# Batch 0 of windowed attention kept in float32 with its turns on TensorE, and constant matmuls in TensorE's gaps before the first feed-forward chunk

## The chip, the cores and the metric

One NeuronCore of a Trainium2 chip runs the kernel. The core has five engines with instruction queues of their own: TensorE (PE, matrix products and transposes), VectorE (DVE), ScalarE (ACT), GpSimd (POOL) and SyncE (SP, which here issues every DMA), and 16 DMA engines. Matrix products are written to PSUM, 8 banks of 128 x 512 float32. The metric is the device time of one execution in microseconds (us); smaller is better.

## What is computed

Eight batches go through an attention with 8 heads of width 64 (512 local and 32 global tokens; a local token sees the 32 global ones and the local ones at most 32 away), then through a Fourier mixing and a feed-forward block. Cut to what matters:

```
s_g   = scale * q_g @ k_all.T ;  out_g = softmax(s_g) @ v_all      # 32 global rows
s_l   = [scale * q_l @ k_g.T , where(|i-j| <= 32, scale * q_l @ k_l.T, -1e9)]
out_l = softmax(s_l) @ [v_g, v_l]                                  # 512 local rows
x     = concat(out_g, out_l)  -> (8, 544, 512)
u     = x + real(fft(fft(x, axis=1), axis=2))
un    = (u - mean(u)) / sqrt(var(u) + 1e-6)
out   = u + relu(un @ w_ch1) @ w_ch2                               # 512 -> 2048 -> 512
```

All of it is held to float32. Most matrix products are made of three float16 products each (high by high, high by low, low by high), for which every operand is first split into a float16 high part and a float16 rest.

## The kernel before, in words

The work is cut into tasks, one method of `Kern` each. `Plan` holds the tasks with an engine, an assumed duration, inputs (`after`), buffers used and made, and a due time. `Plan.order` is a list scheduler: it plays the tasks through a model of the engines, and always starts the task that can start first, ties by class and due time. Due times are propagated back from the consumers and shifted by the table `BIAS`, whose entries were per kind of task and stage. The order that comes out is the order of each engine's queue; nothing is reordered on the chip. Each engine waits on semaphores at the instructions that need another engine's or a DMA's result.

The program has three parts, which overlap:

- **Weights.** 32 tiles of `w_ch1` and `w_ch2` arrive as float64 bit patterns (`w_load`, 512 KB each, L349) and are rebuilt and split on ACT, DVE and POOL (`w_abs`, `w_low`, `w_bits`, `w_join`, `w_hi`, `w_lo`; `w_join` is L373 and L374, `w_bits` L368). `w_scale` 4 needs all 32.
- **Attention**, per batch 4 pairs of heads (p), per pair 2 halves (i) of 256 rows, per half 2 quarters (u) of 128 rows. `scores` (L607 in float32 for batches 0 and 1, L610 in float16 after) writes one bank pair `S` of which there is one. `masked` (DVE, L620) adds the mask, takes the minimum of the negated scaled scores, and copies to `per` (pe). `exps` (ACT, L629), `p_hi` (ACT, L633) and `p_lo` (POOL, L637) make the two float16 parts; `turn` (L642) transposes them by DMA; `values` (PE, L655 and L657) multiplies with the split v (`v_mul`, `v_hi`, `v_lo`, `v_out`); `norm` (DVE, L668) divides; `x_out` (SP, L756) stores. The 32 global rows go the same way in `g_*` tasks, with a DMA transpose in `g_turn` (L714).
- **Fourier mixing** of a batch begins when all of it has been stored: `d_load` (SP, L810 to L812) reloads it, POOL folds it (`d_odd`, L825, to `d_even3`), ACT and DVE split it (`d_hi`, `d_lo`), PE does `d_first` (L920, L922) and `d_second` (L950, L952), and `d_df`, `d_addv`, `d_addp` add the result to a second copy loaded by `load_pair`.
- **Feed-forward** in 17 chunks of 256 rows, two for each batch and a last one of left-over rows. `l_stats` (DVE, L1003), `l_guess`, `l_un` (L1017), `l_hi` (ACT), `l_lo` (DVE, L1026) and `l_turn` (SP, L1032, a DMA transpose for each of two halves) make the split, turned rows `uh`. Then PE does `f_first` (L1058, 192 matmuls in a chunk) and `f_second` (L1076, 96 matmuls), with `f_hi` (L1063) and `f_lo` (L1067) in between.

The first chunk (c = 0) needs the first 256 rows of batch 0, so all of batch 0's attention, its Fourier mixing up to `d_addv` of kt = 0, and the first 16 weight tiles. The `S` bank is a single buffer:

```
        s["S", half] = S = self.psa.tile([P, 2, 512], F32, name="S", tag="A", bufs=1)
```

## Time and profile before

| | us |
|---|---|
| median of 3 runs (1038.67 to 1040.35) | 1039.77 |
| the profiled execution's own time | 1040.43 |
| its span, from the first to the last instruction | 1038.2 |
| TensorE busy in the span | 942.3 |
| VectorE, ScalarE, GpSimd busy | 554.3, 573.0, 592.3 |

The profile is of one execution. Its page gives the busy time of each engine, the span in 40 slices of 26 us, the chain of work that ended last, and groups of instructions by source line with their mean duration, and the idle time before them with what ended it. Rows of the timeline begin with the start and the duration in us. The granted TensorE clock is given as a share of its full speed. Rows of windows give a stretch, its length, and the busy us of PE, PEld (weight loads), DVE, ACT and POOL with instruction counts in brackets, then clock, DMA share and GB/s.

### The profile page before, as it was taken

Reading aid. Unit: us, or ns where it says so; the run is one execution under the profiler, and the core shown is the slowest. Engines: PE = TensorE matmul, PEld = TensorE weight load, DVE = VectorE, ACT = ScalarE, POOL = GpSimd, SP = SyncE. Lnnn points to the kernel's source line nnn. Section 1 sums busy time; section 2 is a strip of 40 time slices with the busy share of each in tenths; the row PEclk is TensorE's granted clock in tenths of the full one; section 3 lists DMA queues with packets and bytes.
Section 4 is the critical chain, followed back from the end, with each engine's and each line's share of the span. In section 5 each row is a group of like instructions: output and inputs, shape, how many; then the busy total and the mean of one; then the engine's idle time right before and its main releaser. Section 6 shows DMA issues by size and latency. Waiting matters only on the chain.

```text
span 1038.2 us, 24797 instructions
## 1 busy us (share of the span) xinstructions
PE 942.3 (91%) x9683; PEld 669.2 (64%) x9683; DVE 554.3 (53%) x1609; ACT 573.0 (55%) x1234; POOL 592.3 (57%) x848
## 2 busy tenths in 40 slices
PE   3854366999999999999999999999999999999996
PEld 2653255667677776677676676777676676767673
DVE  4786899256855485577557557573434324131111
ACT  5996687967686866787777478452122111111110
POOL 4786876896878777969968697781262011010000
PEclk9765556999999999999999999999999999999998
DMA  9999985636786939896795667674230202101000
GB/s 323 246 247 264 285 220 130 133 97 149 153 196 158 224 67 204 147 217 131 146 208 101 185 128 156 135 141 69 57 100 11 62 3 63 42 21 41 1 21 21
DMA packets 249309, 137.59 MB, mean 133 GB/s; under 512 B 200320, under 2 KB 222944, under 8 KB 249192
## 3 DMA queue, kind: packets, MB, share of 16 engines
q1 hardware_dynamic: 249192, 136.00, 56.7%
q8 instruction: 76, 1.25, 0.5%
q14 instruction: 41, 0.34, 0.1%
HBM read 65.10 MB, written 18.35 MB: 80 GB/s over the span
## 4 chain that ended last, share of the span: by engine, by line
PE 71%; DVE 10%; DMA 6%; POOL 5%; ACT 3%; issue 2%; SPq 1%; POOLq 0%; DVEq 0%; ACTq 0%
PE acc L1076 29%; PE ps L1058 29%; PE S L610 3%; DMA pl<-ph 2%; DVE pe L620 2%; PE bk L655 2%; PE psd L950 2%; PE bk L657 2%; PE S L607 2%; DMA raw<-in_moe_w_ch 1%; DVE ps L373 1%; PE psd L920 1%; DMA x<-xs 1%; DMA u<-xs 1%; DVE mx L368 1%
## 5 line engine op out<-in xcount | busy, mean ns | idle before, releaser
L1058 PE MATMUL ps<-uh,wh 128*128 128x256 f16 x3264 | 380.6, 273 | 0.1
L1076 PE MATMUL acc<-wh,h 128*128 128x512 f16 x1632 | 375.1, 379 | 0.8 <-DVE h L1067 0.8
L1058 PEld LDWEIGHTS <-wh 128*128 128x128 f16 x3264 | 315.2, 98 | 51.6 <-issue 0.4
L1076 PEld LDWEIGHTS <-h 128*128 128x128 f16 x1632 | 153.9, 98 | 165.3 <-DVE h L1067 2.0
L1063 ACT ACTIVATE h<-ps 128x512 f16<-128x512 f32 x136 | 80.6, 593 | 268.9 <-PE ps L1058 268.6
L1067 DVE SCALAR_TENSOR_TENSOR h<-ps,h 128x512 f16<-128x512 f32 x136 | 93.6, 688 | 240.3 <-ACT h L1063 240.2
L637 POOL TENSOR_TENSOR ph<-pe,ph 128x448 f16<-128x448 f32 x128 | 132.9, 1054 | 45.1 <-ACT ph L633 39.9
L629 ACT ACTIVATE pe<-pe,nm 128x224 f32<-128x224 f32 x256 | 101.7, 469 | 13.6 <-DVE nm L620 13.6
L620 DVE CUSTOM_DVE_ANT_0 pe<-S,msk,z 128x224 f32<-128x224 f32 x192 | 75.0, 446 | 25.3 <-PE S L610 20.4
L633 ACT ACTIVATE ph<-pe 128x448 f16<-128x448 f32 x128 | 69.3, 564 | 27.7 <-DMA pl<-ph 27.6
L655 PE MATMUL bk<-vN,pl 128*128 128x65 f16 x768 | 69.1, 202 | 13.6 <-DVE x L668 6.2
L974 POOL TENSOR_TENSOR u<-u,asm 128x257 f32<-128x257 f32 x16 | 13.2, 825 | 103.1 <-DMA u<-xs 95.4
L655 PEld LDWEIGHTS <-pl 128*128 128x128 f16 x768 | 60.3, 103 | 14.6 <-DMA pl<-ph 7.6
L657 PEld LDWEIGHTS <-pl 96*128 96x128 f16 x768 | 58.6, 103 | 10.4 <-issue 6.2
L657 PE MATMUL bk<-vB,pl 96*128 96x65 f16 x576 | 52.6, 202 | 0.0
L607 PE MATMUL S<-qk 64*128 64x192 f32 x128 | 30.3, 562 | 22.4 <-DVE nm L620 19.8
L556 POOL TENSOR_TENSOR vN<-vf,vN 128x640 f16<-128x640 f32 x32 | 44.3, 1388 | 9.7 <-ACT vN L552 9.5
L1081 DVE SCALAR_TENSOR_TENSOR u<-acc,ve,u 128x512 f32<-128x512 f32 x34 | 25.4, 748 | 30.9 <-PE acc L1076 30.9
L610 PEld LDWEIGHTS <-qT 64*128 64x128 f16 x1152 | 34.6, 94 | 9.8 <-issue 6.3
L441 POOL TENSOR_TENSOR wh<-wm,wh 128x512 f16<-128x512 f32 x32 | 36.9, 1158 | 6.5 <-ACT wm L434 4.7
L1022 ACT ACTIVATE unh<-un 128x512 f16<-128x512 f32 x34 | 21.2, 624 | 28.0 <-DVE un L1017 27.8
L610 PE MATMUL S<-kT,qT 64*128 64x192 f16 x576 | 36.2, 246 | 0.0
(199 smaller groups left out, 1475.1 us busy)
## 6 DMA issues: line engine op xcount, KB each, us to landing
qk<-in_qk SPq DMA_DIRECT2D x32, 512.0 KB
vf<-in_v SPq DMA_DIRECT2D x32, 320.0 KB
raw<-in_moe_w_ch SPq DMA_DIRECT2D x17, 512.0 KB
xs<-x SPq DMA_DIRECT2D x32, 256.0 KB
out<-u SPq DMA_DIRECT2D x16, 512.0 KB
x<-xs SPq DMA_DIRECT2D x24, 256.0 KB
u<-xs SPq DMA_DIRECT2D x24, 256.0 KB
rw<-in_moe_w_ch SPq DMA_DIRECT2D x8, 512.0 KB
```

The lines of the kernel that those rows point to most:

```text
L607: nc.tensor.matmul(ps, q[r, P * j:P * j + P], kg[r] if o else kw[r, k0:k0 + 192], start=True, stop=True)
L610: nc.tensor.matmul(ps, qT[r, a, j], kg[r, c] if o else kT[r, k0:k0 + 192], start=m == 0, stop=m == 2)
L620: nc.vector.tensor_tensor_reduce(self.per[(4 * p + j) % 4][:, h, 0:224], S[:, h, 224 * n:224 * n + 224], self.msk[:, j], z[:, 8:9], 3e38, ...
L629: nc.scalar.activation(pe[:, h, 0:224], pe[:, h, 0:224], AF.Exp, bias=nm[:, n, h:h + 1], scale=-1.0)
L633: self.nc.scalar.activation(ph[:, 0, :, 0:224], self.per[i % 4][:, :, 0:224], AF.Copy)
L637: self.nc.gpsimd.tensor_sub(ph[:, 1, :, 0:224], self.per[i % 4][:, :, 0:224], ph[:, 0, :, 0:224])
L655: nc.tensor.matmul(pv[:, j % 2, h], pl[:, 4 * a + 2 * h], vN[:, j, c, h, :], start=m == 0, stop=False)
L657: nc.tensor.matmul(pv[:, j % 2, h], pl[0:96, 4 * a + 2 * h + 1], vb, start=False, stop=m == 2)
L1058: nc.tensor.matmul(ps[:, q], wt[:, w, c0:c0 + P], uh[:, :, 4 * a + kt, :], start=n == 0, stop=n == 11)
L1063: self.nc.scalar.activation(h[:, 0], self.fps[c, fp], AF.Relu)
L1067: self.nc.vector.scalar_tensor_tensor(h[:, 1], self.fps.pop((c, fp)), 0.0, h[:, 0], op0=ALU.max, op1=ALU.subtract)
L1076: nc.tensor.matmul(self.acc_f[c, j], h[:, a, q, j * P:(j + 1) * P], self.w[1, f][:, w, :], start=f == 0 and a == 0 and w == 0, stop=f == 1 ...
```

## The change

- **Batch 0 in float32 throughout** (`NRV`). v is no longer scaled and split: `load_v` puts it into a tile with a column of ones, so in pieces of 64 floats for each row and head (for all batches), and `load_vb` loads the shifted copy that `v_out` made. `p_hi`, `p_lo` and `turn` of batch 0's 16 quarters are replaced by `p_turn`, four float32 transposes on PE into PSUM, and `p_copy`, a copy to SBUF on DVE or ACT in turns; `values_raw` does 4 float32 matmuls where there were 12 float16 ones. The same holds for the global rows (`g_turn_raw`, `g_copy`, `g_values_raw`).
- **Masks on TensorE for batches 0 and 1** (`NPM`): the mask is added in `S` by a matmul with a bfloat16 identity, `maxima` on DVE only reduces, and `exps_ps` on ACT reads `S` itself.
- **Fourier banks**: `d_first` and `d_second` take one of three banks in batch 0 (before: two in turn) and one of two after (before: one).
- **First turns on TensorE** (`NLT`): chunks 0 and 1 turn `un` by 4 transposes for each half (`l_pt`), and `l_hi`, `l_lo` split from PSUM into `uh`; the DMA transposes of these two chunks go.
- **Constant matmuls**: until the first `f_first`, the scheduler notes PE's idle time ahead of a task; the methods that open a bank first write up to 12 matmuls of the mask (448 columns or fewer) into the bank that the task then overwrites (`fill`).
- **Order**: assumed durations, `BIAS` (now per kind and stage and per unit of work, some 300 entries) and some sequence constraints are new, so the order on every engine is new.

```
+NRV = 1
+NPM = 2
+NLT = 2
...
+COLD = 1.15
+FILL = 0.24
...
+BIAS = {('load_consts', 0): -10, ('K', 0): 61, ('w_load', 0): 624, ('W', 0): -433, ('w_abs', 0): -2, ('w_low', 0): 180,
...
-                t.dur *= 1.5
+                t.dur *= COLD
+                t.idle = at - free[e]
...
+    def run(self, kern):
         for t in self.order():
+            kern.fills = min(int(t.idle / FILL), 12)
             t.fn(*t.args, *([t.alt] if len(t.alts) > 1 else []))
...
+        self.idh = c.tile([P, P], BF16, name="idh")
+        nc.vector.tensor_copy(self.idh, self.ident)
...
+        self.vf = [c.tile([P, 5, 2, D + 1], F32, name=f"vf{i}") for i in range(4)]
...
-        self.nc.sync.dma_start(s["vf"], self.vd[s["b"], s["hp"]])
+        self.nc.sync.dma_start(s["vf"][:, :, :, 0:64], self.vd[s["b"], s["hp"]][:, 0:5])
+
+    def load_vb(self, p):
+        s = self.st[p]
+        s["vb"] = self.vb[p % NVB]
+        s["v"] = (None, None, self.zc[:, 0:1])
+        self.nc.sync.dma_start(s["vb"][:, :, :, 0:64], self.vd[s["b"], s["hp"], 0:96, 5:8])
...
+        pm = int(s["b"] < NPM)
         s["S", half] = S = self.psa.tile([P, 2, 512], F32, name="S", tag="A", bufs=1)
...
+        self.fill(S[:, 0])
...
+                if pm > o:
+                    for h in range(2):
+                        nc.tensor.matmul(S[:, h, 224 * n:224 * n + 192], self.idh, self.msk[:, j, 0:192], start=False, stop=True)
+
+    def maxima(self, i):
+        nc, (p, half) = self.nc, divmod(i, 2)
+        s = self.st[p]
+        s["nm", half] = nm = self.p2.tile([P, 2, 2], F32, name="nm")
+        S = s["S", half][:, :, 0:448].rearrange("p h (n k) -> p n h k", n=2)
+        nc.vector.tensor_reduce(nm, S, axis=EX, op=ALU.max)
+        nc.vector.tensor_scalar_mul(nm, nm, self.zc[:, 8:9])
+
+    def exps_ps(self, i):
+        nc, (p, half) = self.nc, divmod(i, 2)
+        nm, S = (self.st[p].pop((n, half)) for n in ("nm", "S"))
+        for n in range(2):
+            pe = self.per[(4 * p + 2 * half + n) % 4]
+            for h in range(2):
+                nc.scalar.activation(pe[:, h, 0:224], S[:, h, 224 * n:224 * n + 224], AF.Exp, bias=nm[:, n, h:h + 1], scale=0.125)
 
...
+    def p_turn(self, i, alt):
+        p, j = divmod(i, 4)
+        t = self.bank(alt)
+        self.fill(t)
+        self.st[p]["pt", j] = t = t.rearrange("p (c q) -> p c q", c=4)
+        for h in range(2):
+            for k in range(2):
+                self.nc.tensor.transpose(t[:, 2 * h + k], self.per[i % 4][:, h, P * k:P * k + P], self.ident)
+
+    def p_copy(self, i):
+        p, j = divmod(i, 4)
+        self.st[p]["pl", j] = pl = self.p3.tile([P, 4, P], F32, name="pl")
+        self.copy(i % 2, pl, self.st[p].pop(("pt", j)))
+
+    def copy(self, on_act, o, i):
+        if on_act:
+            self.nc.scalar.activation(o, i, AF.Copy)
+        else:
+            self.nc.vector.tensor_copy(o, i)
+
+    def values_raw(self, i):
+        nc, (p, j) = self.nc, divmod(i, 4)
+        s = self.st[p]
+        pl = s.pop(("pl", j))
+        if j % 2 == 0:
+            s["pv"] = self.bk[:, 0:260].rearrange("p (n h d) -> p n h d", n=2, h=2)
+        pv = s["pv"][:, j % 2]
+        for h in range(2):
+            vb = s["vb"][:, j, h] if j < 3 else s["vf"][0:96, 4, h]
+            nc.tensor.matmul(pv[:, h], pl[:, 2 * h], s["vf"][:, j, h], start=True, stop=False)
+            nc.tensor.matmul(pv[:, h], pl[0:96, 2 * h + 1], vb, start=False, stop=True)
 
...
+        for c in range(5):
+            self.nc.tensor.transpose(t[c // 4][:, P * (c % 4):P * (c % 4) + P], self.pg[:, P * c:P * c + P], self.ident)
...
+    def fill(self, ps):
+
+        n = min(ps.shape[1], 448)
+        m = self.msk.rearrange("p j k -> p (j k)")[:, 0:n]
+        for _ in range(self.fills):
+            self.nc.tensor.matmul(ps[:, 0:n], self.idh[:, 0:ps.shape[0]], m, start=True, stop=True)
+        self.fills = 0
+
+    def bank(self, alt, b=0):
+        if alt == (1 if b else 2):
+            return self.psa.tile([P, 2, 512], F32, name="S", tag="A", bufs=1)[:, 0]
+        return self.ps.tile([P, 512], F32, name="psd", tag="tr" if b else f"acc{alt}")
+
...
+    def l_pt(self, c, j, alt):
+        L = self.L[c]
+        t = self.bank(alt)
+        self.fill(t)
+        L["pt", j] = t = t.rearrange("p (k q) -> p k q", k=4)
+        un = L.pop(("un", j))
+        for k in range(4):
+            self.nc.tensor.transpose(t[:, k], un[:, P * k:P * k + P], self.ident)
+
+    def l_hi_ps(self, c, j):
+        L = self.L[c]
+        if j == 0:
+            L["uh"] = self.p2.tile([P, 2, 8, P], F16, name="uh", tag="uh")
+        self.nc.scalar.activation(L["uh"][:, j, 0:4], L["pt", j], AF.Copy)
+
+    def l_lo_ps(self, c, j):
+        L = self.L[c]
+        self.nc.vector.tensor_sub(L["uh"][:, j, 4:8], L.pop(("pt", j)), L["uh"][:, j, 0:4])
...
+                add(("load_vb", p), SP, .4, self.load_vb, p, new=[vN], kb=150, seq=[("load_v", p)] + prev("load_vb"), **kw)
+                continue
...
+                if b < NPM:
+                    add(("masked", i), DVE, 1.15, self.maxima, i, after=[("scores", i)], use=[S], new=[nm], **kw)
+                    add(("exps", i), ACT, 1.59, self.exps_ps, i, after=[("masked", i)], use=[nm, S], new=pers, **kw)
...
+                    if rv:
+                        pt = ("A", "p", u)
+                        add(("p_turn", u), PE, .6, self.p_turn, u, after=[("exps", i)], seq=[("p_turn", u - 1)] if u else [], use=[per], new=[pt], alts=[["acc0"], ["acc1"], ["A"]], **kw)
+                        add(("p_copy", u), ACT if u % 2 else DVE, .6 if u % 2 else .69, self.p_copy, u, after=[("p_turn", u)], use=[pt], new=[pl], **kw)
+                        add(("values", u), PE, 1.0, self.values_raw, u, after=[("p_copy", u), ("load_v", p), ("load_vb", p)], seq=order, use=[pl, vN, vf, bk], **kw)
+                        continue
...
+            banks = [["tr"], ["A"]] if b else [["acc0"], ["acc1"], ["A"]]
...
+                if c < NLT:
+                    pt = ("A", "l", c, j)
+                    add(("l_pt", c, j), PE, .6, self.l_pt, c, j, after=[("l_un", c, j)], use=[un], new=[pt], alts=[["acc0"], ["acc1"], ["A"]], cls=4)
+                    add(("l_hi", c, j), ACT, .6, self.l_hi_ps, c, j, after=[("l_pt", c, j)], seq=sq, use=[pt] + ([uh] if j else []), new=[] if j else [uh], cls=4)
+                    add(("l_lo", c, j), DVE, .68, self.l_lo_ps, c, j, after=[("l_hi", c, j)], use=[pt, uh], cls=4)
+                    continue
```

The order of the built program at three places. First TensorE's queue at batch 0's second block of scores, before the change (S is the score bank, qk a tile of q and k, gr the global q and k, bk the bank of totals and values):

```order
L607 MATMUL S<-qk_96 128x192 x2
L607 MATMUL S<-gr,qk_96 128x32 x2
L607 MATMUL S<-qk_96 128x192 x2
L607 MATMUL S<-gr,qk_96 128x32 x2
L424 MATMUL bk<-accg,part 128x2
L398 MATMUL vm<-ident,mx_94 1x128
```

And now, with tile numbers and waits; S_235 is the second use of the score bank, msk and idh the mask and the bfloat16 identity, pe the exponentials, psd a bank to turn them in:

```order
L1029 LDWEIGHTS idh_64 [waits DVE_49]
L1029 MATMUL S_235<-msk_63,idh_64 128x448 [waits Activation_49]
...
L648 MATMUL S_235<-qk0_97 128x192 x2
L654 LDWEIGHTS idh_64
L654 MATMUL S_235<-msk_63,idh_64 128x192
...
L648 MATMUL S_235<-gr_162,qk0_97 128x32 x2
L711 MATMUL psd_269<-ident_58,pe0_87 128x128 x4
L711 MATMUL psd_274<-ident_58,pe1_88 128x128 x4
```

Twelve constant matmuls stand ahead of the scores in the same bank, and the first of them waits for ACT, which reads that bank's last scores; in place of float16 products of DMA-turned tiles the transposes follow at once.

Second, SyncE's queue from the transposes ahead of batch 0's last store (L756) to its reload (L810), before:

```order
L642 DMA_TRANSPOSE pl<-ph 128x8x128 x2
L485 DMA qk_98<-in_qk 128x1024
L349 DMA raw<-in_moe_w_ch 128x1024
L642 DMA_TRANSPOSE pl<-ph 128x8x128
L756 DMA xs_135<-x 128x4x128
L489 DMA vf_73<-in_v 128x640
L349 DMA rx<-in_moe_w_ch 128x1024
L349 DMA raw<-in_moe_w_ch 128x1024
L349 DMA rx<-in_moe_w_ch 128x1024 x2
L810 DMA x_1320<-xs_135 128x512
```

Now:

```order
L599 DMA vB_73<-vN 64x780
L600 DMA vB_73<-vN 32x3x260
L521 DMA vf_77<-in_v 128x10x64
L863 DMA xs_147<-xg 64x1x64 x4
L379 DMA raw<-in_moe_w_ch 128x1024
L876 DMA xs_147<-xr 128x4x128
L379 DMA rx<-in_moe_w_ch 128x1024 x2
L930 DMA x_1066<-xs_147 128x512
```

No transpose is left ahead of the reload, and two weight loads instead of four stand between the last store and it; a load of v now has 10 pieces of 64 floats in each partition where it had one of 640.

Third, TensorE's queue at the first chunk, before (vm belongs to the weights' scale):

```order
L610 MATMUL S<-kT_66,qT 128x192
L610 LDWEIGHTS qT
L610 MATMUL S<-kg_68,qT 128x32
...
L407 MATMUL vm<-mxr,part 128x1
L1058 LDWEIGHTS wh
L1058 MATMUL ps_2085<-uh,wh 128x256
```

Now, where un is the chunk's normalised rows, qk_97 belongs to batch 1, and L1209 is the new line of `f_first`:

```order
L1167 MATMUL S<-ident,un 128x128 x4
L1029 LDWEIGHTS idh
L1029 MATMUL psd<-msk,idh 128x448
...
L1167 MATMUL psd<-ident,un 128x128 x4
L648 MATMUL S<-qk_97 128x192 x2
...
L747 MATMUL bk<-vN,pl 128x65
L749 LDWEIGHTS pl
L749 MATMUL bk<-vN,pl 128x65
L1209 LDWEIGHTS wh
L1209 MATMUL ps_1850<-uh,wh 128x256
```

The transposes of the first chunk stand where batch 2's scores (L610) stood, which have moved behind the first chunk's start. Ahead of the first chunk TensorE's queue has 108 constant matmuls, 14 blocks of float32 scores where it had 16, and 24 quarters of values as before (16 of them in float32).

More of the change, by code (lines that the diff above doesn't have):

```diff
@@ L606, in scores @@
                             k0 = SL + P * j - 32
[L607 removed]
+                            nc.tensor.matmul(ps, q[r, P * j:P * j + P], kg[r] if o else kw[r, k0:k0 + 192], start=True, stop=pm <= o)
                         else:
@@ L714, in g_turn, with g_turn_raw, g_copy, g_values_raw @@
         self.nc.sync.dma_start_transpose(pl, self.pgr.rearrange("p a c -> p (a c)"))
+    def g_turn_raw(self, g, alt):
+        if alt:
+            t = [self.ps.tile([P, 512], F32, name="sga", tag=f"acc{j}") for j in range(2)]
+        else:
+            S = self.psa.tile([P, 2, 512], F32, name="S", tag="A", bufs=1)
+            t = [S[:, 0], S[:, 1]]
+        self.G[g] = t
+        self.fill(t[0])
+        for c in range(5):
+            self.nc.tensor.transpose(t[c // 4][:, P * (c % 4):P * (c % 4) + P], self.pg[:, P * c:P * c + P], self.ident)
+    def g_copy(self, g):
+        t = self.G[g]
+        self.G[g] = pl = self.p1.tile([P, 5, P], F32, name="plg")
+        self.copy(1, pl[:, 0:4].rearrange("p c q -> p (c q)"), t[0])
+        self.copy(1, pl[:, 4], t[1][:, 0:P])
+    def g_values_raw(self, g):
+        nc, pl = self.nc, self.G.pop(g)
+        self.G[g] = pv = self.ps.tile([P, 65], F32, name="pvg", tag="tr")
+        for c in range(5):
+            n = P if c < 4 else 96
+            for i in range(2):
+                for h in range(2):
+                    r = slice(64 * i + SG * h, 64 * i + SG * h + SG)
+                    nc.tensor.matmul(pv[r], pl[:n, c, r], self.st[2 * g + i]["vf"][:n, c, h], start=c == 0, stop=c == 4)
     def g_values(self, g):
@@ L1203, in run @@
                     add(("turn", u), SP, 1.3, self.turn, u, after=[("p_lo", u)], seq=pu("turn"), use=[ph], new=[pl], kb=500, **kw)
[L1204 to L1206 removed]
+                    add(("values", u), PE, .43, self.values, u, after=[("turn", u), ("v_out", p)], seq=order, use=[pl, vN, bk], **kw)
+                x = ("qT", "x", p) if rv else ("x", p)
+                add(("norm", i), DVE, .89, self.norm, i, after=[("values", 2 * i), ("values", 2 * i + 1)], use=([bk] if rv else [bk, sc]) + ([x] if half else []), new=[] if half else [x], **kw)
             if p % 2:
                 G, two = ("A", "g", g), (p - 1, p)
[L1209 removed]
+                pg = lambda n: [(n, g - 1)] if g and (n in ("g_scores", "g_exp", "g_values", "g_norm") or g > 2 * NRV) else []
                 if rb:
@@ L1220, in run @@
                 pvg, xg = ("tr", "g", g), ("xg", b)
-                add(("g_values", g), PE, .95, self.g_values, g, after=[("g_turn", g)] + [("v_lo", i) for i in two], seq=pg("g_values"), use=[("plg", g)] + [("vN", i) for i in two], new=[pvg], **kw)
-                add(("g_norm", g), DVE, .7, self.g_norm, g, after=[("g_values", g)], seq=pg("g_norm") if g % 2 else [], use=[pvg, sc] + ([xg] if g % 2 else []), new=[] if g % 2 else [xg], **kw)
+                add(("g_values", g), PE, 1.0 if rv else .95, self.g_values_raw if rv else self.g_values, g, after=gv, seq=pg("g_values"), use=[("plg", g)] + vu, new=[pvg], **kw)
@@ L1226, in run @@
+            add(("x_out", p), SP, .45, self.x_out, p, after=[("norm", 2 * p), ("norm", 2 * p + 1)], use=[x], kb=256, **kw)
         for b in range(B):
@@ L1261, in run @@
                 pre = [base, ("d_tail_lo", b)] + ([("d_first", b, i - 1)] if i else [("load_consts",)])
-                add(("d_first", b, i), PE, .65, self.d_first, b, i, after=pre, use=[eh, ht], new=[ps], **kd)
+                add(("d_first", b, i), PE, .65, self.d_first, b, i, after=pre, use=[eh, ht], new=[ps], alts=banks, **kd)
                 add(("d_z", b, i), ACT, .48, self.d_z, b, i, after=[("d_first", b, i)], use=[ps] + ([] if new else [z]), new=new, **kd)
@@ L1304, in run @@
                 for q in range(2):
-                    add(("f_first", c, fp, q), PE, 1.3, self.f_first, c, fp, q, after=([("f_first", c, fp, 0)] if q else [("l_turn", c, 0), ("l_turn", c, 1)] + col + prv),
+                    add(("f_first", c, fp, q), PE, 1.3, self.f_first, c, fp, q, after=([("f_first", c, fp, 0)] if q else [("l_lo" if c < NLT else "l_turn", c, j) for j in range(2)] + col + prv),
                         use=[uh] + ([ps] if q else []), new=[] if q else [ps], cls=8, due=T)
```

171 lines of the change are left out of this document (101 added, 70 removed).

## The prediction

> **What bounds the kernel now.** I read the page first: its slices, then its queue of transfers.
>
> ```profile
> span 1038.2 us, 24797 instructions
> ...
> PE   3854366999999999999999999999999999999996
> ...
> PEclk9765556999999999999999999999999999999998
> DMA  9999985636786939896795667674230202101000
> ...
> q1 hardware_dynamic: 249192, 136.00, 56.7%
> ```
>
> TensorE is full from the seventh slice to the end. Before that it is half idle, its clock was granted at 0.5 to 0.7 in most slices, and the DMA engines are the row of nines. So the kernel has two parts: a start of some 170 us that ends when TensorE gets its first chunk, and a part in which TensorE's own work sets the end. The windows give the sizes.
>
> ```profile
> 0.00:20.00 20.00, 4.35 (x22) 3.12 (x24) 7.41 (x15) 10.44 (x18) 11.25 (x26) 1.00 0.93 328
> ...
> 0.00:100.00 100.00, 55.25 (x571) 45.12 (x572) 68.50 (x232) 78.53 (x168) 68.34 (x87) 0.75 1.01 269
> 106.00:134.00 28.00, 8.82 (x136) 8.12 (x135) 22.09 (x51) 19.72 (x40) 24.46 (x27) 0.50 0.93 265
> 134.00:170.00 36.00, 21.77 (x238) 17.63 (x237) 34.01 (x84) 28.59 (x67) 26.81 (x33) 0.50 0.82 203
> 170.00:1038.20 868.20, 854.97 (x8721) 597.23 (x8719) 423.81 (x1234) 440.52 (x951) 467.84 (x697) 1.00 0.50 108
> ```
>
> From 170 us on TensorE idles 13.2 us of 868.2, and no other engine is over 54%. In the first 100 us no engine is over 79%, but the DMA share is 1.01. Between 134 and 170 us VectorE is busy 34.0 of 36 us. The timeline gives the milestones of the way to the first chunk.
>
> ```profile
> 99.75 0.58 SPq L756 DMA_DIRECT2D xs<-x  x1
> ...
> 106.66 0.38 SPq L810 DMA_DIRECT2D x<-xs  x1
> ...
> 115.79 2.35 POOL L825 TENSOR_TENSOR s<-x 128x1020 f32<-128x1020 f32 x1 [2.91 <-DMA x<-xs]
> ...
> 133.86 0.41 PE L920 MATMUL psd<-c1r,eh 128*128 128x137 f16 x2 [3.13 <-ACT eh L871]
> ...
> 151.76 0.69 DVE L1003 BATCH_NORM_STATS2 bst<-u 128x6 f32<-128x512 f32 x1
> ...
> 163.90 1.25 SPq L1032 DMA_TRANSPOSE uh<-unh  x1
> ...
> 169.72 2.74 PE L1058 MATMUL ps<-uh,wh 128*128 128x256 f16 x12
> ```
>
> Five steps: (A) batch 0's attention until its reload is issued, 106.7 us; (B) the transfer, 9.1; (C) POOL's fold until the first Fourier matmul, 18.1; (D) until the first row statistics, 17.9; (E) until the first chunk matmul, 18.0. After it (F) 868.5 us of nearly unbroken TensorE. Whatever A to E lose shows at the end, less what TensorE had done before the first chunk and now does after it.
>
> **A, batch 0's attention.** What goes is mostly DMA.
>
> ```profile
> pl<-ph SPq DMA_TRANSPOSE x128
> ...
> uh<-unh SPq DMA_TRANSPOSE x34
> ...
> plg<-pgr SPq DMA_TRANSPOSE x16
> ```
>
> All transfers are 136 MB in 56.7% of 1038.2, so 588.7 us of 16 engines. The first 20 us, nearly all long pieces, moved 6.56 MB in 18.6 us, 2.84 us for a MB. The transposes of these rows are 162 x 0.262 and 16 x 0.328 = 47.7 MB; the other 88.3 MB at 2.84 make 251 us, which leaves 338 us for the transposes: 7.1 us for a MB, 1.86 for a quarter and 2.3 for a global block. Sixteen and two that go from batch 0 are 34 us out of the first 100. Against it, v's loads fall into 256-byte pieces, a form no row shows: seven loads of 0.33 MB ahead of the reload, between nothing more (2.84 a MB) and the transposes' 7.1 a MB, 0 to 10 us; I take 5. Four loads of the shifted v replace four copies of the same 0.15 MB: nothing. DMA is relieved by some 29 us.
>
> The Trainium skill, "DMA: Bandwidth & Descriptors" (Specifications), gives 512 B as the smallest transfer for line rate. It speaks against the new v loads, and by it the end at 7.1 would be nearer, A 5 us later; no run here shows it yet.
>
> VectorE and ScalarE are what can stand next.
>
> ```profile
> L629 ACT ACTIVATE pe<-pe,nm 128x224 f32<-128x224 f32 x256 | 101.7, 469 | 13.6 <-DVE nm L620 13.6
> L633 ACT ACTIVATE ph<-pe 128x448 f16<-128x448 f32 x128 | 69.3, 564 | 27.7 <-DMA pl<-ph 27.6
> ...
> L620 DVE CUSTOM_DVE_ANT_0 pe<-S,msk,zc 128x224 f32<-128x224 f32 x64 | 25.1, 446 | 6.6 <-PE S L607 6.6
> ...
> 95.11 0.69 DVE L368 TENSOR_REDUCE mx<-ps 128x1 f32<-128x512 f32 x1
> ```
>
> ScalarE loses 16 `p_hi` of 69.3/128 = 0.54 (8.7 us) and some v work (5), and gains 8 copies at about the same 0.54 (4.3) and two global copies (2): 78.5 becomes some 71. VectorE's mask step costs 25.1/16 = 1.57 us for a half; the new reduction of 896 columns, by the row of 512, 1.2. Eleven of the old stood ahead of batch 0's last store; eight of the new and eight copies at 0.69 do now, and two more `w_join` (2.8): -17.3 + 9.6 + 5.5 + 2.8 = +0.6. So VectorE still has 69 us ahead of the last store. It cannot be denser than in its own best window (34.01/36 = 0.94) and was 0.79 (22.09/28) in a middling one. From 8 us on, at 0.94, 0.88 and 0.79: the store at 81, 86 or 95 us where it was 99.8. I take 86. The reload stood 6.9 behind the store, for weight loads that waited for their slots; two of four are still there. A = 93, from 86 to 102.
>
> **B** has fewer transfers in the way: 8 (7 to 9). **C.** POOL's fold is unchanged, but TensorE's queue now has three blocks of batch 1's scores and a global one ahead of the first `d_first`, with 32 constant matmuls, and each block waits until ScalarE has read the one before out of the single bank.
>
> ```profile
> 47.61 2.37 PE S L607 x16
> ...
> 1018.40 5.24 PE ps L1058 x48
> 1023.64 5.19 PE acc L1076 x24
> ...
> 24.28 0.37 PE L398 MATMUL vm<-ident,mx 128*1 128x128 f32 x1
> ...
> 35.65 0.69 PE L607 MATMUL S<-qk 64*128 64x192 f32 x4
> ```
>
> 512 columns take 5.19/24 = 0.216 us at full clock, so one constant matmul 0.19, or 0.38 at half. A block costs 2.4 (at half clock) plus masks 0.6, then 1.2 and 1.6 on the other engines, and up to 12 x 0.38 = 4.5 for constants that start only when the bank is free: 10 us, three of them 26 to 30, where the reload, B and the fold leave 32 from the last store. Close to a tie; I add 3: C = 21 (17 to 26). **D** gains from three banks where two were used in turn, and only one block of scores lies between where there were two: 14 (12 to 18).
>
> **E** loses the DMA transpose, 163.90 to 169.72, 5.8 us, for four PE transposes, by 0.37 alone 1.5 at most. But VectorE's new order puts nine tasks between the first and the second `l_un`.
>
> ```profile
> 154.22 1.00 DVE L1017 TENSOR_SCALAR un<-u,mv,ve 128x512 f32<-128x512 f32 x1
> ...
> 157.81 0.83 DVE L1017 TENSOR_SCALAR un<-u,mv,ve 128x512 f32<-128x512 f32 x1
> ...
> 160.88 2.99 DVE L1026 TENSOR_TENSOR unh<-un,unh 128x512 f16<-128x512 f32 x1
> ```
>
> There are 2.6 us between them now; nine tasks of 0.4 to 1.6 are 9. So -5.8 + 1.5 + 6.4, and the 2.99 of a subtraction that is 0.69 elsewhere, less 2.3, and one task fewer behind: E = 17 (12 to 21).
>
> First chunk at 93 + 8 + 21 + 14 + 17 = **153 us**, 16.7 earlier.
>
> **F.** By the order, TensorE has more behind the first chunk's start: two blocks of float32 scores with masks (4 us at full clock), one block and one global block of batch 2 (1.6), a global product (0.5), chunk 1's transposes (1 to 1.5), less some that were there: +6. The first 12 chunk matmuls took 2.74 at half clock and 5.24/4 = 1.31 at full: -1.4, if constants hold the clock. F = 868.5 + 4.6 = 873. Span 1026; the execution's own time was 2.2 over its span and 0.7 over the median: 1026 + 2.2 - 0.7 = **1028**, with A's to E's ends 1012 to 1042.
>
> The Trainium skill, "TensorE: Matmul & The Clock Gate" (Part 1), has the clock at half by default, full after about 3.4 us of sustained work, and half again after an idle window. The clock slices agree as far as they go; by it constants pay only if they leave no such gap, else the start stays at half clock, the second rival.
>
> **Rivals.** *Better:* waits shrink with the DMA queue and A reaches 84, C 17, D 12, E 13: first chunk at 133, 1008. For it speaks the share of 1.01; against it VectorE's 69 us. *Slower, TensorE at half clock is the bound of the start:* its 55.3 us in the first 100 lose 13 (values) and 7 (three score blocks) and gain 42 constants ahead of the reload at 0.38 (16), 74 transposes at 0.2 to 0.37 (15 to 27), 104 float32 products at 0.1 to 0.25 (10 to 26) and masks (5): 81 to 109 us of work for an 86 us stretch. If the clock stays at 0.5, the store comes at 100 to 109, A is 110, C 25, D and E 35 together: first chunk at 178, F 875, **1053**. It decides once blocks of scores take 2.4 and not 1.4 us throughout; against it, a TensorE that is never idle was at full clock (the 0.69 at 35.65). *No change:* A is held by chains of waits, not by DMA, and moves 3 us; D's gain goes into C's queue: 164 to 167, 1038 to 1042. *Starved later:* chunk 2 needs batch 1.
>
> ```profile
> 259.55 7.28 SPq L1032 DMA_TRANSPOSE uh<-unh  x2
> ...
> 269.86 5.40 PE L1058 MATMUL ps<-uh,wh 128*128 128x256 f16 x48
> ```
>
> Its transposes end at 266.8 and chunk 1's last pair begins at 269.9, so it is a few us ahead of need. An earlier first chunk leaves more of batch 1 and 2 to POOL and ScalarE behind it: a stall of 5 to 12 us, 1033 to 1040.
>
> **How the numbers follow.** Forecast 0.45, better 0.15, no change 0.12, starved 0.12, half clock 0.16. The range leaves out the half-clock case and the best of "better": 1008 to 1046. A measurement of this kernel tells some 0.2%, 2 us, from no change. Faster by more: 0.45 + 0.15 + 0.08 (starved) + 0.05 (of no change) = 0.73; within it 0.08; slower 0.16 + 0.03 = 0.19.
>
> **What would show it.** A: the last `x_out` of batch 0 at about 86 us, the reload at 93. C: the wait before `d_first` ends with DVE's or ACT's split (the fold was late) or with TensorE's own queue (the scores were). E: `l_un` to `l_un` 9 us apart, no DMA behind `l_lo`. F: 873 us with under 15 us idle. Wrong if the clock is at 0.5 up to the first chunk, if the store does not move, or if TensorE idles for several us around chunk 2.

## The result, and the profile after

The change made the kernel slower, by 0.9%.

| | before | after |
|---|---|---|
| median, us | 1039.65 (1037.91 to 1040.35, a disturbed run left out) | 1049.79 (1043.16 to 1054.36, 10 runs) |
| ratio to before, 95% interval | | 1.0086 [1.0066, 1.0107] |
| the profiled execution, its span | 1040.43, 1038.2 | 1045.1, 1043.3 |
| first chunk matmul | 169.7 | 168.7 |
| from there to the end | 868.5 | 874.6 |

The timeline after, at the milestones of the prediction (start, duration, queue or engine, line):

```profile
95.61 0.38 SPq L876 DMA_DIRECT2D xs<-xr  x1
...
100.00 0.33 SPq L930 DMA_DIRECT2D x<-xs  x1
...
107.37 2.34 POOL L945 TENSOR_TENSOR s<-x 128x1020 f32<-128x1020 f32 x1 [2.77 <-DMA xf<-xs]
...
150.91 0.68 DVE L1135 BATCH_NORM_STATS2 bst<-u 128x6 f32<-128x512 f32 x1
...
168.70 3.55 PE L1209 MATMUL ps<-uh,wh 128*128 128x256 f16 x31
```

Batch 0's last store came 4.1 us earlier, its reload 6.7 earlier, and all of that was lost again before the first Fourier matmul at 136.6 (before 133.9). The windows from 8 us to the first chunk matmul, and behind it, of before and then of after:

```profile
8.00:169.70 161.70, 87.00 (x962) 71.75 (x962) 128.98 (x373) 129.19 (x279) 117.18 (x129) 0.63 0.97 257
169.70:1038.20 868.50, 855.27 (x8722) 597.46 (x8721) 424.11 (x1235) 440.79 (x953) 468.08 (x698) 1.00 0.50 108
```

```profile
8.00:168.70 160.70, 120.69 (x971) 80.54 (x971) 124.02 (x276) 104.83 (x222) 73.84 (x91) 0.79 0.71 201
168.70:1043.30 874.60, 862.54 (x8872) 600.75 (x8869) 424.98 (x1239) 457.13 (x992) 479.35 (x711) 0.99 0.52 112
```

What the change was to do, it did: the DMA share of the start fell from 0.97 to 0.71, POOL's and ScalarE's work by 43 and 24 us, and the granted clock rose from 0.63 to 0.79. Only the time did not follow. The chain from the reload on shows why. First TensorE, then ScalarE of the kernel after:

```profile
102.15 3.15 PE L1029 MATMUL S<-msk,idh 128*128 128x448 bf16 x8 [1.52 <-ACT pg L797]
105.23 0.69 PE L648 MATMUL S<-qk 64*128 64x192 f32 x4
...
111.34 4.56 PE L1029 MATMUL S<-msk,idh 128*128 128x448 bf16 x12 [3.79 <-ACT pe L670]
115.83 0.60 PE L648 MATMUL S<-qk 64*128 64x192 f32 x4
...
121.38 4.63 PE L1029 MATMUL S<-msk,idh 128*128 128x448 bf16 x12 [3.32 <-ACT pe L670]
125.94 0.60 PE L648 MATMUL S<-qk 64*128 64x192 f32 x4
...
128.69 1.08 PE L777 MATMUL sga<-qk,gr 128*64 128x512 f32 x4
...
136.61 0.55 PE L1051 MATMUL psd<-c1r,eh 128*128 128x137 f16 x3
```

```profile
119.86 1.46 ACT L670 ACTIVATE pe<-S,nm 128x224 f32<-128x224 f32 x4 [4.94 <-DVE nm L662]
...
133.09 0.78 ACT L796 ACTIVATE pg<-sga,ng,zc 128x512 f32<-128x512 f32 x1 [7.42 <-DVE ng L791]
...
134.58 0.71 ACT L991 ACTIVATE eh<-x,dsc 128x514 f16<-128x514 f32 x1
```

L1029 are the constants, L648 a block of scores, L670 the exponential that reads the block out of the bank, L796 batch 1's second global exponential, L991 the split of the folded batch 0. The bracket at the second row of constants is the thing to see: TensorE stood idle for 3.79 us until ScalarE had read the bank, and **only then** ran 4.56 us of constants, with the block of scores behind them. The idle time that they were to fill was over when they began, since they write the very bank that the block waits for. So a block follows the one before it by 10 us (105.23, 115.83, 125.94), and the global block follows three of them. ScalarE, in order, stands 7.42 us at L796, and the split behind it starts at 134.58, although POOL had folded the even half by 119.07:

```profile
118.34 0.73 POOL L968 TENSOR_TENSOR x<-x 128x256 f32<-128x256 f32 x1
...
122.95 0.71 POOL L983 TENSOR_TENSOR s<-s 128x256 f32<-128x256 f32 x1
```

### The profile page after: what moved, and what is told of

It reads as the page before. It is cut to its first block, busy times and chain, and to the rows that moved or that the text cites. A ratio compares the mean times of both kernels' runs of the same rounds, so it can differ in the third digit from the quotient of the medians.

```text
span 1043.3 us, 24847 instructions
## 1 busy us (share of the span) xinstructions
PE 983.2 (94%) x9837; PEld 681.3 (65%) x9837; DVE 556.0 (53%) x1516; ACT 564.2 (54%) x1216; POOL 560.6 (54%) x833
## 4 chain that ended last, share of the span: by engine, by line
PE 87%; DVE 8%; ACT 2%; POOL 1%; issue 1%; DMA 0%; SPq 0%; ACTq 0%; DVEq 0%; POOLq 0%
PE acc L1227 34%; PE ps L1209 33%; PE S L651 3%; PE S L1029 3%; PE bk L747 2%; PE S L648 2%; PE bk L749 2%; DVE nm L661 1%; PE S L1082 1%; DVE mx L398 1%; PE psd L1082 1%; DVE ps L403 1%; DVE wm L404 1%; PE psd L1051 1%; ACT pe L670 1%
## 5 line engine op out<-in xcount | busy, mean ns | idle before, releaser
L1209 PE MATMUL ps<-uh,wh 128*128 128x256 f16 x3264 | 382.4, 273 | 1.1 <-DVE h L1218 1.1
L1209 PEld LDWEIGHTS <-wh 128*128 128x128 f16 x3264 | 313.4, 98 | 52.4 <-issue 2.3
L697 POOL TENSOR_TENSOR ph<-pe,ph 128x448 f16<-128x448 f32 x112 | 116.2, 1052 | 51.5 <-ACT ph L693 50.0
L689 ACT ACTIVATE pe<-pe,nm 128x224 f32<-128x224 f32 x192 | 76.3, 469 | 16.1 <-DVE nm L680 16.0
L693 ACT ACTIVATE ph<-pe 128x448 f16<-128x448 f32 x112 | 60.2, 565 | 8.1 <-DMA pl<-ph 8.0
L747 PE MATMUL bk<-vN,pl 128*128 128x65 f16 x672 | 55.5, 195 | 1.0 <-DVE x L760 0.5
L747 PEld LDWEIGHTS <-pl 128*128 128x128 f16 x672 | 49.1, 99 | 5.6 <-DMA pl<-ph 0.8
L1029 PE MATMUL S<-msk,idh 128*128 128x448 bf16 (+1 forms) x78 | 28.6, 539 | 23.8 <-ACT pe L670 12.6
L749 PEld LDWEIGHTS <-pl 96*128 96x128 f16 x672 | 47.0, 98 | 3.9 <-issue 0.5
L749 PE MATMUL bk<-vB,pl 96*128 96x65 f16 x504 | 42.9, 195 | 0.0
L1029 PEld LDWEIGHTS <-idh 128*128 128x128 bf16 x108 | 14.3, 134 | 43.1 <-issue 27.2
L758 DVE TENSOR_SCALAR dn<-bk,z 128x4 f32<-128x4 f32 x56 | 12.1, 217 | 45.1 <-PE bk L749 45.0
```

The costliest lines, as they stand in the source:

```text
L689: nc.scalar.activation(pe[:, h, 0:224], pe[:, h, 0:224], AF.Exp, bias=nm[:, n, h:h + 1], scale=-1.0)
L693: self.nc.scalar.activation(ph[:, 0, :, 0:224], self.per[i % 4][:, :, 0:224], AF.Copy)
L697: self.nc.gpsimd.tensor_sub(ph[:, 1, :, 0:224], self.per[i % 4][:, :, 0:224], ph[:, 0, :, 0:224])
L747: nc.tensor.matmul(pv[:, j % 2, h], pl[:, 4 * a + 2 * h], vN[:, j, c, h, :], start=m == 0, stop=False)
L749: nc.tensor.matmul(pv[:, j % 2, h], pl[0:96, 4 * a + 2 * h + 1], vb, start=False, stop=m == 2)
L1029: self.nc.tensor.matmul(ps[:, 0:n], self.idh[:, 0:ps.shape[0]], m, start=True, stop=True)
```

## The experiments

Two theories. **W**: the constants wait with the product that they stand before, and what they take is added to the chain from block to block. **K**: the clock that they hold is worth their time, and the loss is elsewhere; of these the likeliest was **Q**, the order on ScalarE and VectorE. Each time is a median with the lowest and the highest run, then the ratio to runs of the kernel before on the same chip (medians 1039.1 to 1040.5 there) with its 95% interval. Milestones are from one profiled execution, and executions of one kernel differ by up to 15 us, so a milestone says less than a median.

**No constants.**

```
-        for _ in range(self.fills):
+        for _ in range(0):
```

> All 108 constant matmuls are left out; the order of everything else is that of the change. Theory W (the constants write the bank that the score block behind them waits for, so they start when the wait is over and lengthen the chain from block to block by all they take): first block of scores at some 8 us instead of 12.9, reload at 92 to 95 instead of 100.0, first Fourier matmul at 122 to 126 instead of 136.6, first chunk matmul at 153 to 158 instead of 168.7, time 1030 to 1036. Theory K (the clock that the constants hold is worth what they cost): TensorE falls to 0.5 for most of the first 160 us, its float32 blocks take 3.8 instead of 2.2 us, reload at 100 or later, first chunk matmul at 168 or later, time 1045 or more.

1033.83 us (1028.09 to 1036.33), ratio 0.9951 [0.9931, 0.9970]: 14 us (by the ratios) to 16 (by the medians) under the change, and faster than before. The same place in TensorE's and ScalarE's timeline:

```profile
94.07 1.01 PE L648 MATMUL S<-qk 64*128 64x192 f32 x4 [1.51 <-ACT pg L797]
...
100.91 1.01 PE L648 MATMUL S<-qk 64*128 64x192 f32 x4 [3.01 <-ACT pe L670]
...
107.93 1.01 PE L648 MATMUL S<-qk 64*128 64x192 f32 x4 [3.20 <-ACT pe L670]
...
119.50 0.41 PE L1051 MATMUL psd<-c1r,eh 128*128 128x137 f16 x2 [4.88 <-ACT eh L991]
```

```profile
117.24 0.78 ACT L796 ACTIVATE pg<-sga,ng,zc 128x512 f32<-128x512 f32 x1 [4.43 <-DVE ng L791]
...
118.73 0.71 ACT L991 ACTIVATE eh<-x,dsc 128x514 f16<-128x514 f32 x1
```

Here the clock is at half (1.01 for four products that took 0.60 above), K's case exactly, and still the blocks stand 7 us apart and not 10. The reload is issued at 92.47 and the first chunk matmul starts at 153.8, as W had it; the first Fourier matmul at 119.5 is sooner than W's 122 to 126. From reload to first Fourier matmul it is 27.0 us; the expectations further down count from 91 and say 28.4.

```profile
92.47 0.33 SPq L930 DMA_DIRECT2D x<-xs  x1
```

**No constants ahead of blocks of scores.**

```
-        self.fill(S[:, 0])
+        self.fills = 0
```

> Only the constants ahead of blocks of scores go (60 of 108); those ahead of global scores, turns, Fourier products and the chunk's transposes stay. Theory W: within 3 us of the kernel without any constants, first Fourier matmul at 123 to 128, time 1031 to 1038. Theory K: blocks of scores at half clock, 3.8 us each, time 1043 or more.

1035.75 (1027.10 to 1042.55), 0.9944 [0.9922, 0.9967]: as without any. The constants ahead of scores are the ones that cost (the built kernel lacks 59 of the 108). The milestone was missed: the first Fourier matmul came at 130.0 and not at 123 to 128, in an execution whose clock stood at 0.50 from 40 to 70 us.

**Half of them.**

```
-            kern.fills = min(int(t.idle / FILL), 12)
+            kern.fills = min(int(t.idle / FILL), 12) // 2
```

> The change with half as many constants at each place (rounded down, at most 6). If the constants' own time is what is paid (W), the time lies half way between the change (1049.8) and the kernel without any (1033.8): 1039 to 1044, first Fourier matmul at 126 to 130. If a few constants are enough for the clock and only the many are too much, it is at or under the kernel without any: 1030 to 1035.

1043.32 (1039.12 to 1052.01), 1.0041 [1.0017, 1.0065], between the two, as W had the time. The milestone was missed here too: first Fourier matmul at 135.8 and not at 126 to 130. In this execution the blocks of scores ran at half clock from 44.7 us on (1.01 for four products), in that of the change from 66.6 on. That half the constants cost half is read from the medians alone.

**The constants alone, in the kernel before**, 106 by the same rule, its order untouched.

```
-                t.dur *= 1.5
+                t.dur *= 1.5; t.idle = at - free[e]
...
+            kern.fills = min(int(t.idle / 0.24), 12); t.fn(*t.args, *([t.alt] if len(t.alts) > 1 else []))
...
+        self.fill(S[:, 0])
...
+        self.G[g] = sg, s2 = t[0], t[1][:, 0:SG]; self.fill(sg)
```

> The kernel before with nothing but the constants: by the same rule of the planner's idle time, 106 of them ahead of blocks of scores, global scores and Fourier products, in the bank that the product behind them is about to write (identity copied by ScalarE). Its order is that of the kernel before. W: the constants start when the bank is free and are paid there, less what the DMA queue hides: reload from 106.7 to 110 to 120, first chunk matmul from 169.7 to 175 to 185, time 1045 to 1056. K: its start runs at 0.5 to 0.6 of the clock, constants raise that, products shorten: first chunk matmul at 160 to 168, time 1030 to 1038.

1053.81 (1048.83 to 1056.89), 1.0133 [1.0107, 1.0160]. The window up to its first chunk matmul:

```profile
8.00:178.70 170.70, 99.10 (x1068) 68.16 (x1068) 127.53 (x373) 128.68 (x279) 116.61 (x129) 0.70 0.95 242
```

The clock rose from 0.63 to 0.70, and the first chunk matmul moved 9 us back. So the two parts of the change add up: constants +14.6 on the old kernel and +14 to 16 on the new one, the rest -5.3. The Trainium skill, "TensorE: Matmul & The Clock Gate" (Part 1), lets the clock rise after some 3.4 us of sustained work; by that rule constants raise the clock, and they did, by 0.07 in both kernels (0.63 to 0.70 here, 0.72 to 0.79 from the change without constants to the change). The time went the other way. Sustained work did not always raise it: a row in the next section has TensorE busy for 10 us at 0.50.

**The same constants in an idle bank.**

```
-        self.fill(S[:, 0])
+        self.fill(self.bank(0) if self.fills else S[:, 0])
```

> As many constants at the same places, but those ahead of a block of scores write one of the accumulator banks, which is idle there, and not the bank of scores: they can run while the block waits. Theory W: the three blocks of batch 1 come 3 to 4 us apart less each, first Fourier matmul at 124 to 128, first chunk matmul at 156 to 160, time 1032 to 1038. Theory K: as the change or 1 to 2 us better, since the clock is the same: 1043 to 1050. Theory Q (the fold's split stands in ScalarE's queue behind batch 1's second global exponential, and that is late with or without constants): first Fourier matmul at 132 or later, 1043 or more.

1039.33 (1031.98 to 1045.72), 0.9996 [0.9969, 1.0023], first Fourier matmul at 122.8: two thirds of the loss come back by the bank alone, against K and Q, but not all; the time is 1 us above W's range. In this kernel the twelve constants ahead of the very first block still wait, for the copy of the identity, and that block begins at 12.4; without constants it begins at 6.2, and its first masks run at 8.3. The next pair takes this out: constants only from the end of batch 0 on, and the identity copied by ScalarE.

```
-            kern.fills = min(int(t.idle / FILL), 12)
+            kern.fills = min(int(t.idle / FILL), 12) if t.at > 84 else 0
...
-        nc.vector.tensor_copy(self.idh, self.ident)
+        nc.scalar.activation(self.idh, self.ident, AF.Copy)
...
-        self.fill(S[:, 0])
+        self.fill(self.bank(0) if self.fills else S[:, 0])
```

The last edit is in the first of the two only. (`t.at > 84` is the planner's own clock.)

> The change with constants only from the end of batch 0's attention on (66 of 108: 32 ahead of batch 1's three blocks of scores, the others ahead of Fourier products and chunk turns), those ahead of the blocks in an idle accumulator bank; identity copied by ScalarE. If the bank is what costs (W): blocks of batch 1 5.5 to 6.5 us apart, from the reload's issue to the first Fourier matmul 26 to 29 us as without constants (28.4), first chunk matmul 151 to 158, time 1029 to 1035. If running them costs wherever they write: 32 to 36 us, time 1038 to 1044.

> The same 66 constants, those ahead of the blocks in the bank of scores as in the change. W: blocks of batch 1 9 to 10.5 us apart, from the reload's issue to the first Fourier matmul 34 to 38 us (36.6 to 37.5 in the change), first chunk matmul 160 to 166, time 1038 to 1045. If the bank does not matter: within 3 us of the kernel that writes the idle bank.

Idle bank 1032.41 (1024.32 to 1036.71), 0.9897 [0.9859, 0.9935]; bank of scores 1038.82 (1031.41 to 1041.14), 0.9980 [0.9960, 1.0001]. The two intervals do not meet. The first is the fastest kernel of this study; its interval overlaps that of the kernel without constants, so it is not shown that constants in an idle bank gain anything. The second block of batch 1 in TensorE's timeline, idle bank first:

```profile
103.24 2.44 PE L1029 MATMUL psd<-msk,idh 128*128 128x448 bf16 x12
107.91 0.60 PE L648 MATMUL S<-qk 64*128 64x192 f32 x4 [2.23 <-ACT pe L670]
```

```profile
111.85 4.32 PE L1029 MATMUL S<-msk,idh 128*128 128x448 bf16 x12 [5.04 <-ACT pe L670]
116.10 0.60 PE L648 MATMUL S<-qk 64*128 64x192 f32 x4
```

In the first the constants run inside the wait and the block starts when the bank is free; in the second the same twelve start after it. An idle bank does not make them free for certain: ahead of the third block they took 4.60 us from 111.08 on, and the block began at 115.62, 1.4 us after the exponential had been done with the bank (at 114.23).

The times came as W had them. The milestones did not, in both kernels: from reload to first Fourier matmul 33.1 us and not 26 to 29, and 39.2 and not 34 to 38; blocks 7.4 and 7.7 us apart in the idle bank, 13.1 and 10.0 in the bank of scores; first chunk matmul at 164.4 and 168.8, both later than foreseen. The difference between the two, 6.1 us to the first Fourier matmul, fits the 6.4 between the medians. One reason for the idle bank's lateness is in the last section.

The medians also part the cost. The kernel with the 66 late constants in the bank of scores is 11 us faster than the change, so the other 42, ahead of batch 0's last store, cost more; against the kernel without constants whose identity ScalarE copies, too (1034.44, below), the 66 cost 4.4, with intervals that just meet.

**Batch 1's third block and second global block behind the Fourier products**, constants as in the change (a pass over the planned order: these tasks and all that hang on them are put behind `d_z2` 3).

```
+    late, one, two = {("scores", 10), ("g_scores", 3)}, [], []
+    for t in ts[a:z]:
+        if t.key in late or late & set(t.after):
...
+    return ts[:a] + one + two + ts[z:]
```

> All constants stay; batch 1's third block of scores and second global block, with all that hangs on them, are issued behind the five first Fourier products of batch 0 instead of ahead of them. Theory Q (the order on ScalarE and VectorE holds the split of the fold): the split of the even half at 119 to 123 instead of 134.6, first Fourier matmul at 126 to 129 instead of 136.6, first chunk matmul at 158 to 162, time 1036 to 1041. Theory W alone (constants, wherever they stand): the block's constants only move behind the Fourier products and are paid there, first chunk matmul at 165 or later, time within 4 us of the change.

1056.19 (1049.65 to 1059.12), 1.0146 [1.0118, 1.0174]: slower still, by more than the 4 us that W allowed. From reload to first Fourier matmul 30.4 us and not 36.6, but from there to the first row statistics 27.3 and not 14.3: the block with its twelve constants stands between the Fourier stages now. **The same with the global block alone, without constants** (`late` holds `("g_scores", 3)` only):

> No constants, and batch 1's second global block (its scores, maxima, exponential, pair and turn) issued behind the five first Fourier products of batch 0. In the kernel without constants ScalarE's queue stands at that global exponential until 117.24 and the split of the even half, whose fold is done some 6 us before, is behind it. If the order on ScalarE holds it (Q): split 4 to 6 us sooner after the fold's start (21.3 us after it now), first chunk matmul 150 to 152, time 1028 to 1032. If the time only moves into the Fourier products (as with the block of scores in the kernel that put the fold first): first row statistics at 135 as now, time 1032 to 1037.

1038.75 (1033.83 to 1045.06), 0.9989 [0.9970, 1.0008]: first Fourier matmul at 116.4 and not 119.5, row statistics at 141.5 and not 134.9, later than either case foresaw. Q falls in both. ScalarE's queue is where the delay is seen; moving the late task only moves the delay.

**DMA turns put back beside TensorE's**, without constants.

```
-        self.fill(t)
+        self.nc.sync.dma_start_transpose(self.kT[i % 2][:, 0:1024].rearrange("p (c q) -> p c q", c=8), self.phr[i % NPH].rearrange("p a h c -> p (a h c)"))
```

> No constants; beside each of the 16 turns that TensorE makes for batch 0 a DMA transpose of the same size is issued again, of zeros that nothing reads. This puts back the 30 us of DMA that the prediction counted (16 x 1.86) and the 16 issues on SyncE, and no wait of the attention on them. If batch 0 was held by DMA (step A's reason), its last store goes from 88 to 95 to 102 and the time to 1040 to 1048. If DMA was only busy and it was the round trip of each block through pair and transpose that held batch 0, the last store stays within 4 us of 88 and the time within 4 of 1033.8.

1044.74 (1044.54 to 1046.92), 1.0053 [1.0038, 1.0068], 10 to 11 us over the two kernels without constants (1033.83, and 1034.44 with ScalarE's identity). The last store of batch 0 came at 101.43. In the profiled executions of those two, in the same order, it came at 87.97 and at 93.27, with a mean clock from 20 to 60 us of 0.90 and 0.68, here 0.83; so some 8 us of the distance are not the clock. SyncE's queue, ScalarE and VectorE with the 16 turns:

```profile
80.08 4.51 SPq L707 DMA_TRANSPOSE kT<-ph  x3
84.68 0.53 SPq L379 DMA_DIRECT2D raw<-in_moe_w_ch  x1
```

```profile
89.18 0.62 ACT L387 ACTIVATE ps<-raw 128x512 f32<-128x512 f32 x1 [7.20 <-DMA raw<-in_moe_w_ch]
```

```profile
89.83 0.69 DVE L398 TENSOR_REDUCE mx<-ps 128x1 f32<-128x512 f32 x1 [6.28 <-ACT ps L387]
...
100.32 0.22 DVE L758 TENSOR_SCALAR dn<-bk,zc 128x4 f32<-128x4 f32 x1 [1.20 <-PE bk L734]
```

No instruction of batch 0's attention waits for these turns. But a load of weights is issued behind the last of them, ScalarE and VectorE stand 7.20 and 6.28 us for it, and batch 0's last division (L758) stands behind that step in VectorE's queue; with ScalarE's identity and no turns VectorE has no such wait. So turns by DMA delay batch 0, in this order by way of the weights, and step A's reason, less DMA, is borne out. What their transfers and what their issues on SyncE each lost was not taken apart.

**Single parts undone**, without constants: batch 0 by pairs and DMA turns (`NRV = 0`), chunks turned by DMA (`NLT = 0`), masks on VectorE (`NPM = 0`).

> No constants, and batch 0's values and probabilities again as pairs of float16 with the DMA turns (masks on TensorE for two batches and the first chunks' turns on TensorE stay; the planner orders anew). If batch 0 was held by its transposes and pairs (step A of the prediction), the reload goes from 91 to 100 to 108 and the time from 1033.8 to 1042 to 1052. If it was held by VectorE's weights and masks alone, reload within 4 us of 91, time within 4 of 1033.8.

> No constants, and the first two chunks turned by DMA again. The prediction put the gain of TensorE's turns at 5.8 - 1.5 = 4.3 us less what else is late: first chunk matmul 3 to 5 us later after the first row statistics (18.9 in the kernel without constants), time 1036 to 1039. Rival: nothing, since the row statistics and the order of VectorE set that stretch: within 2 us of 1033.8.

> No constants, and the masks of batches 0 and 1 added by VectorE again (1.57 us for each half block instead of the maxima's 1.1 to 1.3), TensorE free of 32 mask products of batch 0 and as many of batch 1. If VectorE bounds batch 0, 8 half blocks cost 8 x 0.3 = 2 to 4 us and the time is 1036 to 1039; if the single bank of scores bounds it, VectorE's old step frees the bank without waiting for ScalarE's exponential (1.46 us less each), three blocks of batch 1 come 1.5 us sooner each, and the time is 1029 to 1033.

1065.01, 1072.88 and 1073.77 us, far outside every range above. These decide little, for the planner orders anew and its table was fitted to another set of tasks. With DMA turns in batch 0 the reload comes at 136.2, later than in the kernel before, which makes these operations in an order made for them. The other two lose it long behind the parts that they undo: 909 and 917 us behind the first chunk matmul where 872.5 were. For the chunk turns:

```profile
161.30:1070.60 909.30, 873.41 (x8861) 609.78 (x8859) 428.50 (x1240) 453.70 (x989) 478.99 (x709) 0.97 0.50 108
```

TensorE's work is nearly the same (862.61 without constants), with 36 us of gaps, most of them between 400 and 500 us. One thing can be read ahead of that: from first row statistics to first chunk matmul it took 17.4 us with DMA turns, 18.9 with TensorE's. So no gain of TensorE's turns is seen there, though the two orders differ.

**The identity copied by ScalarE**, without constants (the edit stands above).

> No constants, and the float16-like copy of the identity matrix that masks and constants multiply with is made by ScalarE and not by VectorE, where the one copy of 128 x 128 stood for 6.1 us, from 2.1 to 8.2, while POOL set 3.5 and 2.05 us of zeros. If POOL's work held it: a copy of under 0.5 us, first mask product at 7.3 instead of 8.3, time the same or 1 us less (1031 to 1035). If the copy is slow in itself: some us on ScalarE too.

1034.44 (1027.71 to 1041.85), 0.9937 [0.9912, 0.9963]: the first masks run at 7.7 and not at 8.3, the time is the same.

## Why the prediction was wrong

Its terms, with the profiled executions of the change and of two kernels without constants, the second with ScalarE's copy of the identity:

| | predicted | after | without constants | the same, ScalarE's identity |
|---|---|---|---|---|
| A, until the reload is issued | 93 | 100.0 | 92.5 | 97.9 |
| B + C, until the first Fourier matmul | 29 | 36.6 | 27.0 | 27.0 |
| D, until the first row statistics | 14 | 14.3 | 15.4 | 16.4 |
| E, until the first chunk matmul | 17 | 17.8 | 18.9 | 18.9 |
| F, from there on | 873 | 874.6 | 872.5 | 873.9 |
| span | 1026 | 1043.3 | 1026.3 | 1034.1 |

**The step that failed is the price of the constants**, in A, where they had no term, and in C, where they were given 3 us as a tie; they cost 14 us by the ratios and 16 by the medians. The sum for everything else came out within 2 us in every term of the first kernel without constants. Part of that is luck: that execution is the fastest of its seven, 5.7 us under their median, and the median itself is 6 us over the 1028 foreseen. The second column without constants, an execution near its kernel's median, has A 5 us and D 2 us above the forecast.

- **A** had 13.7 us from less DMA. The direction was right: last store foreseen at 86, at 87.97 and 93.27 without constants, 101.43 with the turns put back. Its sum had no term for constants, though 42 of them stand in that stretch; they were counted in the half-clock rival only. After, the first two blocks start at 12.9 and 23.0, without constants at 6.2 and 14.3. The 8.7 us lost by the second block are more than the 7.6 at the last store (95.6 to 88.0).
- **B** was 7.4 us (8 foreseen). **C** was sized as a tie between TensorE's queue and POOL's fold and given 3 us. The text even said that constants start when the bank is free, and that a block could cost 10 us, three of them 26 to 30, against 32 from the last store. Both sides were off. From the last store at 95.6 the fold took 28 us (to 123.66) and not 32. The blocks took 26 from 102.15 to 128.2, as the 26 to 30 had it, but they did not begin at the last store: they began when a global exponential had freed the bank, and the second global block came behind them, so ScalarE reached the split 39 us after that store. There was no tie.
- **D** and **E** were as foreseen in size. E's reason was half right: the second `l_un` followed the first by 10.3 us (9 foreseen) and cancels what TensorE's turns save, and the kernel with DMA turns, in another order, was no later there.
- **F** grew by 6.1 us (4.6 foreseen), by more work of TensorE behind the first chunk. The rival "starved later" did not come: TensorE idles 12 us in all behind the first chunk, before 13.
- The rival "half clock" was the nearest in time (1053), for another reason. Its mechanism, blocks at half clock, is what the kernel without constants has, at 0.51 from 69 to 114 us, and it is 14 to 16 us faster.
- Two slips in the working changed nothing here: TensorE is full from the eighth slice on, not the seventh, and the ends of A to E, all taken at once, give 1009 and 1051 and not 1012 and 1042.

The median of after is 5 us over its profiled execution, which the prediction had no term for. The runs of one kernel spread over 11 us and more (the kernel before beside the experiments over up to 10, 1037.85 to 1047.85), and the longer ones have the lower mean clock: 1043.16 at 0.966, 1054.36 at 0.949; in the idle-bank kernel 1024.32 at 0.967, 1036.71 at 0.957. Two traces with the same order up to batch 0's reload show how: the change, and then the kernel with the fold first, from 40 to 60.

```profile
40.00:60.00 20.00, 16.50 (x143) 13.06 (x142) 19.38 (x43) 16.28 (x35) 6.27 (x9) 1.00 0.55 160
```

```profile
40.00:60.00 20.00, 17.93 (x113) 13.70 (x112) 16.60 (x36) 13.84 (x30) 4.75 (x7) 0.70 0.48 132
```

In the second the clock fell at 48 us and not at 61, and batch 0's last store came at 102.4 and not 95.6. So the time of the start hangs on when the clock falls in that run. What makes it fall sooner in one run than in another was not tried. The prediction's argument against the half clock, that a TensorE that is never idle was at full clock, does not hold in every run: in the kernel with ScalarE's identity the profile has it busy without a gap, and at half. What keeps the clock there was not tried either.

```profile
40.00:50.00 10.00, 10.00 (x51) 8.34 (x50) 7.08 (x17) 5.49 (x11) 0.00 (x0) 0.50 0.38 117
```

## What to carry to other kernels

Work that is to fill an engine's gap must need nothing that the gap waits for: constants for the clock, if there are to be any (no run here shows that they gain), go into memory that nobody holds, and a trace shows at once whether they start at the beginning of the wait or at its end. A higher granted clock and busier slices are no gain in themselves; look at the distance from block to block. A change of two parts is priced part by part, and a fitted table of orders can make a single part that is undone look worse than it is, so the part is taken out with the order kept.

## What was not expected of the hardware

The one copy of the identity on VectorE took 6.13 us, and the same copy on ScalarE 0.31. VectorE and POOL of the kernel after, then ScalarE of the one with the copy there:

```profile
2.11 6.13 DVE L291 CAST idh<-ident 128x128 bf16<-128x128 f32 x1
...
2.22 2.05 POOL L331 MEMSET kT<- 128x1152 f16 x2
4.21 3.51 POOL L332 MEMSET ph<- 128x4096 f16 x1
7.66 0.27 POOL L335 MEMSET vN<- 128x10 f16 x4
7.81 0.34 POOL L361 MEMSET zr<- 64x274 f16 x1
```

```profile
2.01 0.31 ACT L291 ACTIVATE idh<-ident 128x128 bf16<-128x128 f32 x1
```

The copy on VectorE lasts as long as POOL's row of zeros, to 8.2 us. In the idle-bank kernel VectorE's step of 128 x 4 in `maxima`, 0.23 at best, took 4.22 us beside POOL's `p_lo`, and the global maxima that ScalarE's split stood behind came 4 us later for it:

```profile
119.02 4.22 DVE L662 TENSOR_SCALAR nm<-nm,zc 128x4 f32<-128x4 f32 x1
```

```profile
120.21 3.98 POOL L697 TENSOR_TENSOR ph<-pe,ph 128x448 f16<-128x448 f32 x4
```

The Trainium skill, "SBUF — State Buffer" (SBUF: two separate sides), says that VectorE, for some forms of instruction, and GpSimd share one pair of ports, which one instruction holds until it ends while the other engine waits. These rows fit that, and go further: VectorE seems to have waited through several instructions of POOL, one behind the other. It does not always: at 112.33 the same step took 0.35 us, with POOL busy on either side of it. That the copy is not slow in itself is shown on ScalarE only; that POOL held VectorE was read off the trace in both cases.
